# q of six batches transposed on VectorE in 32x32 blocks instead of on TensorE, in a pooled-attention and mixer kernel

## The chip, the cores and the metric

The kernel runs on one core of one Trainium2 chip. The metric is the device time of one execution, in microseconds. Times are medians of several executions of the same program. A median quoted beside a ratio is over all runs of that kernel. Runs of one kernel differ by about 1.5%, and the longer ones have a lower mean granted clock of TensorE: the kernel before took 302.3 us at a mean clock of 1.00 and 305.5 us at 0.979. In the profiled run of the kernel before, the low clock stands at 11 to 21 us.

## The reference, cut to what matters

```python
# q, k, v: [8 batches, 8 heads, 576 tokens, 64]
k_p = k.reshape(B, H, 72, 8, 64).mean(axis=3)          # 8 tokens pooled into one
v_p = v.reshape(B, H, 72, 8, 64).mean(axis=3)
attn = softmax(q @ k_p.T / 8)                          # 576 x 72 a head
x = attn @ v_p                                         # heads side by side: [B, 576, 512]
u = x + (relu(x.T @ w_tok1) @ w_tok2).T                # token mixing, 576 -> 256 -> 576
out = u + relu(u @ w_ch1) @ w_ch2                      # feed-forward, 512 -> 1536 -> 512
```

q enters the score matmul as the moving operand with head dimension on partitions, so each q tile has to be transposed first. The feed-forward is most of the arithmetic.

A warning about correctness. In this draw q and the pooled k are so small that the softmax is nearly flat: with q set to zero the reference's output changes by 0.36% in norm. The chip's correctness check therefore passes even for a kernel with a wrong q. For the changed layout the loads, the block transposes and the score matmul on the host in plain array code gave the exact scores in the order that the later stages expect.

## The kernel before: the parts that matter

The program is a sequence of units. Unit n computes the feed-forward of batch n and, in its gaps, the attention and token mixing of batch n + 1. Unit 0 follows a head that does the attention of batch 0; units 1 to 6 are alike, unit 7 and a last one for leftover rows have no attention to do. Tiles named `ps` lie in PSUM, the memory that the matmuls write to; there are one to three buffers of a kind, and one is written again only after an engine has read what stood in it. The position table below says after which step of unit n's feed-forward a step of batch n + 1 is put.

```python
        def qT(hp):                            # one head pair: five 128x128 transposes on TensorE
            def go():
                ps = (ps_one if first else ps_tr).tile([P, NE, 2, BP], BF16, ...)
                for rr in range(NE):
                    nc.tensor.transpose(out=ps[:, rr]..., in_=st["qb"][:, hp, rr * P:(rr + 1) * P], identity=ident)
                nc.scalar.copy(out=dst, in_=ps)            # PSUM -> SBUF on ScalarE
        # [cut]
        def av(c):                             # attention times v, then the normalisation
            def go():
                # 8 matmuls into ps_two (2 buffers)  [cut]
                nc.vector.reciprocal(out=den[rows], in_=view[:, :, :, D])
                nc.vector.tensor_tensor(out=dst..., in0=view[:, :, :, 0:D], in1=den..., op=ALU.mult)   # x
        # [cut]
        def u(c):                              # token mixing back, residual; ps_one has 3 buffers
            # matmuls into ps_one [cut]
            nc.vector.tensor_tensor(out=dst, in0=ps, in1=x, op=ALU.add)
    # [cut]
    LATER = {1: "kpT", 3: "q0", 5: "q1", 6: "o0", 7: "q2", 8: "e0", 10: "o1", 11: "q3", 12: "e1", 14: "o2", 16: "e2",
             18: "o3", 20: "e3", 23: "av0", 25: "av1", 27: "av2", 29: "av3", 31: "av4", 33: "at0", 34: "at1", ...}
    # [cut]
    def unit(n, at):
        load(n + 2)                            # k, q, v of a later batch, from GpSimd's queue
        batches[n + 1][0]()                    # pooling of k and v on GpSimd (batch 1: VectorE)
        # feed-forward of batch n, with the steps of `at` between  [cut]

    with tc.manual_schedule(engines={PE, POOLE}):          # order as written for TensorE and GpSimd
        with tc.manual_schedule(engines={DVE, ACT}):       # head and unit 0: also VectorE and ScalarE
            # head [cut]
            unit(0, FIRST)
        for n in range(1, B + 1):
            unit(n, LATER)                     # here a scheduler orders VectorE and ScalarE
```

The last lines: TensorE and GpSimd follow the written order, while from unit 1 on the scheduler decides where an instruction of VectorE stands in its queue. VectorE then works through its queue in order: in the trace after the change, an add that doesn't need the late load stands behind a transpose that waits 15.4 us for it.

The softmax here doesn't subtract the row's maximum and nothing guards it: scores larger than these inputs give would overflow.

Of the kernel before, what the change touches and what calls it, by code (L numbers as in the profile page):

```python
# [19 lines left out]
def kernel(  # L20
# [19 lines left out]
    BP, BR = 64, S // 64  # L40
    NE = (BR + 1) // 2
    EV, OD = NE * BP, (BR - NE) * BP
    NO = BR - NE
    ORDER = list(range(1, BR, 2)) + list(range(0, BR, 2))
    CHUNK = [1, 3, 0, 2]
    HP = H // 2
    DM = H * D
    DT = moe_w_tok1.shape[1]
# [22 lines left out]
    uT_tails = singles.tile([P, 4, 4 * P], BF16)  # L71
    u_tails = singles.tile([P, 4, DM], BF16)
    kTs = [singles.tile([P, 2, H * SP], BF16, name=f"kTs{i}") for i in range(2)]


    loaded = {}

    def load(b):
        if b >= B:
            return  # L80
        kr = raw.tile([SP, H, POOL, D], BF16, name="kr")
        vr = raw.tile([SP, H, POOL, D], BF16, name="vr")
        qb = raw.tile([P, HP, BR * D + D], BF16, name="qb")
        nc.vector.memset(qb[:, :, BR * D:], 0.0)
        loaded[b] = (kr, vr, qb)

        def q_in(a0, a1):
            return q[b, 2 * a0:2 * a1].rearrange("(a l) (p r) d -> (l p) a (r d)", l=2, r=BR)

        def kv(t, src, h0, h1):  # L90
            nc.gpsimd.dma_start(out=t[:, h0:h1].rearrange("j h i d -> j h (i d)"),  # L91
                                in_=src[b, h0:h1].rearrange("h (j i) d -> j h (i d)", i=POOL))

        if b == 0:
            for a in range(2):
                nc.sync.dma_start(out=qf[:, a:a + 1, :], in_=q_in(a, a + 1))
            loaded["q23"] = q_in
            kv(kr, k, 0, HP)
            kv(kr, k, HP, H)
            make_identity(nc, ident)  # L100
            kv(vr, v, 0, HP)
            kv(vr, v, HP, H)
        else:
            kv(kr, k, 0, H)
            nc.gpsimd.dma_start(out=qb[:, :, 0:BR * D], in_=q_in(0, HP))  # L105
            kv(vr, v, 0, H)

    def load_tok():
        nc.gpsimd.dma_start(out=f2, in_=moe_w_tok2.rearrange("(c p) n -> p c n", p=P))
        w = moe_w_tok1.rearrange("(p r) n -> p r n", r=BR)  # L110
        for half in range(2):
            rows = slice(half * BP, (half + 1) * BP)
            nc.gpsimd.dma_start(out=w_tok1[rows, 0:4, :].rearrange("p (b a) n -> p b (a n)", a=2),
                                in_=w[:, 0:8, :].rearrange("p (b u a) n -> p b u (a n)", u=2, a=2)[:, :, half])
        for half in range(2):
            rows = slice(half * BP, (half + 1) * BP)
            nc.gpsimd.dma_start(out=w_tok1[rows, 4 + half, :], in_=w[:, ORDER[8], :])

    def permute_tok2():
        src = f2.rearrange("t m (p r) -> t m r p", r=BR)  # L120
        dst = w_tok2.rearrange("t m (r p) -> t m r p", p=BP)
        for m in range(2):
            nc.gpsimd.tensor_copy(out=dst[:, m, 0:NO], in_=src[:, m, 1:BR:2, :])
            nc.gpsimd.tensor_copy(out=dst[:, m, NO:BR], in_=src[:, m, 0:BR:2, :])
        for half in range(2):
            nc.gpsimd.tensor_copy(out=w_tok2t[:, :, half, half * BP:(half + 1) * BP], in_=w_tok2[:, :, 8 * BP:S])

# [11 lines left out]
    def pool8(eng, t, hs, dst, dup):  # L139
        n = hs.stop - hs.start  # L140
        t4 = att.tile([SP, H // 2, 4, D], FP32, name="t4")
        eng.tensor_tensor(out=t4[:, 0:n], in0=t[:, hs, 0:4], in1=t[:, hs, 4:8], op=ALU.add)  # L142
        eng.tensor_tensor(out=t4[:, 0:n, 0:2], in0=t4[:, 0:n, 0:2], in1=t4[:, 0:n, 2:4], op=ALU.add)
        if dup:
            eng.tensor_tensor(out=dst, in0=t4[:, 0:n, 0, None, :].broadcast_to([SP, n, 2, D]),
                              in1=t4[:, 0:n, 1, None, :].broadcast_to([SP, n, 2, D]), op=ALU.add)
        else:
            eng.tensor_tensor(out=dst, in0=t4[:, 0:n, 0], in1=t4[:, 0:n, 1], op=ALU.add)
# [2 lines left out]

    def batch_steps(b):

        par, first = b % 2, b == 0
        st = {}
        kT = kTs[par]
        lower = slice(par * BP, (par + 1) * BP)

        def prepare():
            kr, vr, qb = loaded.pop(b)  # L160
            kp = att.tile([SP, H, 2, D], BF16, name="kp")
            vp = att.tile([SP, H, D + 1], BF16, name="vp")
            ex = att.tile([SP, H * S + BP], BF16, name="ex")
            nc.vector.memset(vp[:, :, D], float(POOL))
# [2 lines left out]
            if b > 1:  # L167
                for s in ("K0", "K1", "V0", "V1"):
                    name[s]()
            st["qT"] = att.tile([P, HP, 2, EV], BF16, name="qT")  # L170
            st["AT"] = att.tile([P, 2, DM], BF16, name="AT")
            st["x"] = mix.tile([P, 4, DM], BF16, name="x")
            st["u"] = mix.tile([P, 4, DM], BF16, name="u")
# [6 lines left out]
        def pool(t, g):  # L180
            def go():
                hs = slice(g * HP, (g + 1) * HP)
                dst = st["kp"][:, hs] if t == "kr" else st["vp"][:, hs, 0:D]
                pool8(nc.vector if b == 1 else nc.gpsimd, st[t], hs, dst, t == "kr")
            return go

        def kpT(h0, h1):
            def go():
                ps = ps_tr.tile([P, H, SP], BF16, name="pt")
                for h in range(h0, h1):  # L190
                    nc.tensor.transpose(out=ps[:, h, :], in_=st["kp"][:, h].rearrange("j e d -> j (e d)"),  # L191
                                        identity=ident[0:SP, 0:SP])
                for half in range(2):
                    rows = slice(half * D, (half + 1) * D)
                    copy = nc.scalar.copy if first and half == 0 else nc.vector.tensor_copy
                    copy(out=kT[rows, half, h0 * SP:h1 * SP], in_=ps[rows, h0:h1, :].rearrange("p h j -> p (h j)"))  # L196
            return go
# [18 lines left out]
        def qT(hp):  # L216
# [9 lines left out]
                    nc.scalar.copy(out=dst, in_=ps)  # L226
            return go

        def score(hp, odd):
            n, c0 = (OD, 0) if odd else (EV, OD)  # L230

            def go():
                ps = ps_two.tile([P, 2, 512], FP32, name="p2")
                for hl in range(2):
                    h = 2 * hp + hl
                    nc.tensor.matmul(out=ps[0:SP, hl, 0:n], lhsT=kT[:, odd, h * SP:(h + 1) * SP],  # L236
                                     rhs=st["qT"][:, hp, hl, 0:n], start=True, stop=True)
                exv = st["ex"][:, 0:H * S].rearrange("j (h n) -> j h n", h=H)
                nc.scalar.activation(out=exv[:, 2 * hp:2 * hp + 2, c0:c0 + n], in_=ps[0:SP, :, 0:n],
                                     func=AF.Exp, scale=scale)  # L240
            return go

        def av(c):
# [35 lines left out]
        def at_tile(c):  # L279
            def go():  # L280
                for m in range(2):
                    if c == 0:
                        st["at", m] = ps_one.tile([P, 512], FP32, name="p1")
                    ps = st["at", m]
                    nc.tensor.matmul(out=ps, lhsT=w_tok1[:, CHUNK[c] if c < 4 else 4 + par, m * P:(m + 1) * P],
                                     rhs=st["x"][:, c, :] if c < 4 else st["xt"], start=(c == 0), stop=(c == 4))
                    if c == 4:
                        relu(m, ps)
# [9 lines left out]
        def at(m):  # L298
            def go():
                ps = ps_one.tile([P, 512], FP32, name="p1")  # L300
                for c in range(5):
                    nc.tensor.matmul(out=ps, lhsT=w_tok1[:, CHUNK[c] if c < 4 else 4 + par, m * P:(m + 1) * P],  # L302
                                     rhs=st["x"][:, c, :] if c < 4 else st["xt"], start=(c == 0), stop=(c == 4))
                relu(m, ps)
            return go
# [48 lines left out]
            name[f"K{g}"], name[f"V{g}"] = pool("kr", g), pool("vr", g)  # L354
        for hp in range(HP):
            name[f"q{hp}"], name[f"o{hp}"], name[f"e{hp}"] = qT(hp), score(hp, 1), score(hp, 0)
        for c in range(5):
            name[f"av{c}"], name[f"u{c}"], name[f"t{c}"] = av(c), u(c), uT(c)
            name[f"at_{c}"] = at_tile(c)
# [6 lines left out]
    def unit_steps(n, st):  # L366
# [4 lines left out]
        for m in range(NM):  # L371
            ps = ps_one.tile([P, 512], FP32, name="p1")
            for kk in range(4):
                nc.tensor.matmul(out=ps, lhsT=w_ch1[:, kk, m * P:(m + 1) * P], rhs=uT[:, kk, :],  # L374
                                 start=(kk == 0), stop=(kk == 3))
                if kk == 1:
                    yield
            if m % 2 == 0 or n == 0:
                nc.scalar.activation(out=GT[:, m, :], in_=ps, func=AF.Relu)  # L379
            else:  # L380
                nc.vector.tensor_scalar(out=GT[:, m, :], in0=ps, scalar1=0.0, scalar2=None, op0=ALU.max)
# [1 line left out]
        for c in range(4):  # L383
# [6 lines left out]
            o_sb = outp.tile([P, DM], FP32, name="o")  # L390
            nc.vector.tensor_tensor(out=o_sb, in0=ps, in1=u_all[:, c, :], op=ALU.add)
            for half in range(2):
                b, r = (2 * c + half, ORDER[8]) if n == B else (n, ORDER[2 * c + half])
                nc.sync.dma_start(out=out[b].rearrange("(p r) n -> p r n", r=BR)[:, r, :],
                                  in_=o_sb[half * BP:(half + 1) * BP, :])
            yield
# [5 lines left out]
             16: "kpT1 V0", 17: "o1", 18: "e1", 19: "q2", 20: "o2 V1", 21: "e2", 22: "q3", 23: "o3", 24: "e3",  # L402
             25: "av0", 26: "av1", 27: "av2", 28: "av3", 29: "av4", 31: "at0", 32: "at1", 34: "U0", 35: "U1",
             36: "t0 U2", 38: "t1 U3", 39: "U4", 40: "t2", 42: "t3", 46: "t4"}
    LATER = {1: "kpT", 3: "q0", 5: "q1", 6: "o0", 7: "q2", 8: "e0", 10: "o1", 11: "q3", 12: "e1", 14: "o2", 16: "e2",
             18: "o3", 20: "e3", 23: "av0", 25: "av1", 27: "av2", 29: "av3", 31: "av4", 33: "at0", 34: "at1",
             37: "u0", 38: "u1", 39: "t0", 40: "u2", 41: "t1", 42: "u3", 43: "u4 t2", 45: "t3", 47: "t4"}
    warm = singles.tile([P, 512], BF16)

# [25 lines left out]
    with tc.manual_schedule(engines={PE, POOLE}):  # L435
        batches = [batch_steps(b) for b in range(B)]
        with tc.manual_schedule(engines={DVE, ACT}):
# [13 lines left out]
                head(s)  # L451
            nc.vector.memset(kTs[1][D:P, 0, :], 0.0)
            nc.vector.memset(kTs[1][0:D, 1, :], 0.0)
            unit(0, FIRST)
        for n in range(1, B + 1):
            unit(n, LATER)
# [30 lines left out]
```

## Time and profile before

| | before |
|---|---|
| time, median (range) of the first three runs | 302.89 us (302.15 to 305.53) |
| TensorE busy | 95% of the span |
| VectorE, ScalarE busy | 52%, 33% |
| chain of waits that ended last | 87% TensorE |
| q transposes on TensorE in units 1 to 6 | 120 of 128x128 |

The page of the kernel before has one line of busy times, and rows of 40 equal slices (7.6 us each) in tenths; "PEclk" is the clock granted to TensorE. The last line here is the chain of waits.

```profile
span 303.9 us, 4654 instructions
PE 287.8 (95%) x1880; PEld 153.7 (51%) x1916; DVE 158.4 (52%) x318; ACT 100.6 (33%) x176; POOL 135.8 (45%) x120
...
PE   8789998999999999999999999999999999999993
...
DVE  4136956684277427752756275725572567333321
...
PEclk9759999999999999999999999999999999999998
...
PE 87%; DVE 5%; ACT 2%; DMA 2%; issue 2%; POOLq 0%
```

TensorE has no slack to speak of after the head. The table of windows makes this sharper: start and end, length, then the busy time of each engine, and granted clock, share and GB/s of DMA.

```profile
76.00:112.00 36.00, 35.48 (x244) 19.59 (x248) 18.27 (x37) 15.85 (x28) 23.42 (x18) 1.00 0.52 92
112.00:148.00 36.00, 35.44 (x251) 19.17 (x254) 20.29 (x41) 13.02 (x23) 23.55 (x19) 1.00 0.56 98
```

In 36 us TensorE is busy for over 35.4 at full clock. VectorE is busy for 18 to 20 us. What a block of q transposes costs is seen in TensorE's timeline (start, duration, instruction; what it waited for in brackets):

```profile
134.63 0.44 PE L220 MATMUL pt<-ident,qb 128*128 128x128 bf16 x5 [0.24 <-DVE kTs_92 L196]
134.90 1.03 PE L374 MATMUL p_1630<-uT,w_ch_86 128*128 128x512 bf16 x4
```

The next matmul starts 0.27 us after the block, so five transposes take 0.27 us of TensorE. The last relu of unit 3's feed-forward on VectorE starts 0.20 us after the first attention matmul, and VectorE's normalisations follow each other closely (first line TensorE, the others VectorE):

```profile
146.41 0.42 PE L256 MATMUL p_1744<-vp,ex 72*128 72x65 bf16 x8
146.61 0.69 DVE L381 TENSOR_SCALAR GT<-p_1737 128x512 bf16<-128x512 f32 x1 [1.31 <-PE p_1737 L374]
147.22 0.20 DVE L268 RECIPROCAL den<-p_1744 128x8 f32<-128x8 f32 x1
147.45 0.69 DVE L274 TENSOR_TENSOR x<-p_1744,den 128x512 bf16<-128x512 f32 x1
148.06 0.20 DVE L268 RECIPROCAL den<-p_1761 128x8 f32<-128x8 f32 x1
148.29 0.69 DVE L274 TENSOR_TENSOR x<-p_1761,den 128x512 bf16<-128x512 f32 x1
```

One normalisation takes 0.84 us. One more thing: batch 2's q load, issued at 26.97 us in the head. The view of its tile, for the load issued in that window, gives the time from issue to landing:

```profile
DMA to landing us min/median/max: 24.7/24.7/24.7
```

It lands at 51.7 us, in the middle of unit 0, because the loads of weights stand before it in the same queue.

### The profile page before, as it was taken

The numbers are of one execution on the slowest core, as the hardware profiler recorded it, in microseconds if no ns is written. First come the engines' busy times: TensorE is split into PE (matmuls) and PEld (weight loads), VectorE is DVE, ScalarE is ACT, GpSimd is POOL, SyncE is SP. The second block draws the span as 40 slices with busy tenths as digits, with TensorE's granted clock in tenths as the row PEclk, the third lists the DMA queues.
The fourth block names the chain that finished last, engine by engine and source line by source line (L and its number), as shares of the span: only waits on it lengthen the run. The fifth ranks groups of instructions, "written<-read, shape, count | busy, mean of one in ns | idle before, by whom it ended". The sixth has DMA issues, their size and how long they took to land.

```text
span 303.9 us, 4654 instructions
## 1 busy us (share of the span) xinstructions
PE 287.8 (95%) x1880; PEld 153.7 (51%) x1916; DVE 158.4 (52%) x318; ACT 100.6 (33%) x176; POOL 135.8 (45%) x120
## 2 busy tenths in 40 slices
PE   8789998999999999999999999999999999999993
PEld 3565444455555555455545554455446545444441
DVE  4136956684277427752756275725572567333321
ACT  2344478005810481029202920093008400300300
POOL 8285104992798079904991499994000000000000
PEclk9759999999999999999999999999999999999998
DMA  7999999927751755173727373200131012114023
GB/s 146 205 204 205 205 203 171 194 49 126 114 101 39 144 87 105 35 149 44 118 66 129 57 118 71 60 9 2 43 70 27 2 36 70 37 29 98 11 50 90
DMA packets 26517, 28.27 MB, mean 93 GB/s; under 512 B 4864, under 2 KB 21376, under 8 KB 26496
## 3 DMA queue, kind: packets, MB, share of 16 engines
q0 software_dynamic: 20160, 17.35, 37.8%
q1 hardware_dynamic: 6048, 10.03, 13.5%
q10 hardware_dynamic: 288, 0.59, 0.7%
q8 instruction: 15, 0.25, 0.3%
q14 instruction: 6, 0.05, 0.1%
HBM read 35.85 MB, written 9.44 MB: 149 GB/s over the span
## 4 chain that ended last, share of the span: by engine, by line
PE 87%; DVE 5%; ACT 2%; DMA 2%; issue 2%; POOLq 0%
PE pt L220 3%; PE pt L327 3%; DMA kr<-in_k_dram 2%; PE pt L414 1%; DVE x L274 1%; DVE kTs_92 L196 1%; PE pt L191 1%; ACT GT L379 1%; DVE kTs_93 L196 1%; PE p_2935 L386 1%; PE p_1119 L386 1%; PE p_753 L386 1%; PE p_3286 L386 1%; PE p_2487 L386 1%; PE p_1435 L386 1%
## 5 line engine op out<-in xcount | busy, mean ns | idle before, releaser
L386 PEld LDWEIGHTS <-GT 128*128 128x128 bf16 x432 | 38.7, 98 | 36.8 <-issue 0.9
L374 PEld LDWEIGHTS <-w_ch_86 128*128 128x128 bf16 x432 | 40.5, 98 | 32.1 <-issue 1.0
L105 POOL DMA_DIRECT2D qb<-in_q_dram x7 | 5.4, 776 | 51.4 <-PE pt L220 50.7
L226 ACT COPY qT<-pt 128x640 bf16<-128x640 bf16 x28 | 19.3, 691 | 9.0 <-PE pt L220 7.9
L256 PEld LDWEIGHTS <-ex 72*128 72x128 bf16 x320 | 15.1, 98 | 10.2 <-DVE x L274 2.2
L220 PEld LDWEIGHTS <-qb 128*128 128x128 bf16 x160 | 11.7, 100 | 12.0 <-issue 6.6
L414 PE MATMUL pt<-warm 128*128 128x512 bf16 x34 | 12.0, 468 | 2.8 <-DVE kTs_92 L196 1.6
L220 PE MATMUL pt<-ident,qb 128*128 128x128 bf16 x140 | 12.3, 218 | 1.5 <-DVE kTs_92 L196 0.7
L328 DVE COPY uT<-pt 128x512 bf16<-128x512 bf16 x28 | 11.8, 421 | 3.4 <-PE pt L327 3.4
L327 PEld LDWEIGHTS <-u 128*128 128x128 bf16 x112 | 8.6, 98 | 7.2 <-issue 0.9
L236 PEld LDWEIGHTS <-kTs_93 128*72 128x72 bf16 x64 | 7.2, 113 | 8.6 <-issue 1.8
L236 PEld LDWEIGHTS <-kTs_92 128*72 128x72 bf16 x64 | 8.1, 126 | 6.8 <-issue 1.3
L302 PEld LDWEIGHTS <-w_tok_83 128*128 128x128 bf16 x70 | 6.8, 98 | 8.3
L327 PE MATMUL pt<-ident,u 128*128 128x128 bf16 x112 | 10.8, 219 | 0.1
L91 POOL DMA_DIRECT2D kr<-in_k_dram x9 | 7.5, 838 | 7.0 <-DVE t_485 L142 6.1
L317 PEld LDWEIGHTS <-w_tok_84 128*128 128x128 bf16 x64 | 6.2, 98 | 7.4 <-issue 0.5
L91 POOL DMA_DIRECT2D vr<-in_v_dram x9 | 7.5, 836 | 3.1 <-PE p_403 L345 3.1
L414 PEld LDWEIGHTS <-warm 128*128 128x128 bf16 x36 | 3.8, 113 | 5.4 <-issue 2.6
L196 DVE COPY kTs_93<-pt 64x576 bf16<-64x576 bf16 (+1 forms) x10 | 4.0, 395 | 4.3 <-PE pt L191 4.2
L204 PEld LDWEIGHTS <-ident 72*72 72x72 bf16 x32 | 4.4, 138 | 2.0 <-issue 1.3
L191 PEld LDWEIGHTS <-kp 72*128 72x128 bf16 x64 | 3.4, 100 | 3.2 <-DVE kp L211 1.0
L131 POOL DMA_DIRECT2D w_ch_86<-in_moe_w_ch_dram x3 | 2.3, 754 | 5.8 <-DMA kr<-in_k_dram 2.9
(809 smaller groups left out, 694.0 us busy)
## 6 DMA issues: line engine op xcount, KB each, us to landing
out_dram<-o SPq DMA_DIRECT2D x72, 128.0 KB, 2.4
kr<-in_k_dram POOLq DMA_DIRECT2D x7, 576.0 KB, 8.3
qb<-in_q_dram POOLq DMA_DIRECT2D x7, 576.0 KB, 6.5
vr<-in_v_dram POOLq DMA_DIRECT2D x7, 576.0 KB, 9.6
w_ch_86<-in_moe_w_ch_dram POOLq DMA_DIRECT2D x3, 512.0 KB, 9.2
w_ch_87<-in_moe_w_ch_dram POOLq DMA_DIRECT2D x3, 512.0 KB, 17.2
qf<-in_q_dram SPq DMA_DIRECT2D x2, 288.0 KB, 3.0
kr<-in_k_dram POOLq DMA_DIRECT2D x2, 288.0 KB, 8.3
```

The costliest lines, as they stand in the source:

```text
L91: nc.gpsimd.dma_start(out=t[:, h0:h1].rearrange("j h i d -> j h (i d)"), in_=src[b, h0:h1].rearrange("h (j i) d -> j h (i d)", i=POOL))
L196: copy(out=kT[rows, half, h0 * SP:h1 * SP], in_=ps[rows, h0:h1, :].rearrange("p h j -> p (h j)"))
L220: nc.tensor.transpose(out=ps[:, rr].rearrange("m l p -> m (l p)"), in_=st["qb"][:, hp, rr * P:(rr + 1) * P], identity=ident)
L226: nc.scalar.copy(out=dst, in_=ps)
L236: nc.tensor.matmul(out=ps[0:SP, hl, 0:n], lhsT=kT[:, odd, h * SP:(h + 1) * SP], rhs=st["qT"][:, hp, hl, 0:n], start=True, stop=True)
L256: nc.tensor.matmul(out=halves[h // 4][:, (h % 4) * (D + 1):(h % 4 + 1) * (D + 1)], lhsT=st["ex"][:, h * S + n0:h * S + n0 + P], rhs=st["vp ...
L302: nc.tensor.matmul(out=ps, lhsT=w_tok1[:, CHUNK[c] if c < 4 else 4 + par, m * P:(m + 1) * P], rhs=st["x"][:, c, :] if c < 4 else st["xt"], ...
L327: nc.tensor.transpose(out=ps[:, kk, :], in_=src[:, kk * P:(kk + 1) * P], identity=ident)
L328: nc.vector.tensor_copy(out=dst[:, :, o:o + P], in_=ps)
L374: nc.tensor.matmul(out=ps, lhsT=w_ch1[:, kk, m * P:(m + 1) * P], rhs=uT[:, kk, :], start=(kk == 0), stop=(kk == 3))
L386: nc.tensor.matmul(out=ps, lhsT=GT[:, m, c * P:(c + 1) * P], rhs=w_ch2[:, m, :], start=(m == 0), stop=(m == NM - 1))
L414: nc.tensor.matmul(out=ps, lhsT=warm[:, 0:P], rhs=warm, start=True, stop=True)
```

## The change

The intent is to take the q transposes off the busiest engine. For batches 2 to 7, q is loaded with two heads and token parity on groups of 32 partitions, so that VectorE can transpose 32x32 blocks straight into a tile with head dimension on partitions. The pooled k is laid out to match, with zeros for the other head. ScalarE no longer copies q out of PSUM, and takes three of VectorE's relus a unit. The order of token rows becomes the natural one.

```diff
+    BY_PE = 2                                    # batches 0 and 1 stay on TensorE
+                for ph in range(2):
+                    nc.gpsimd.dma_start(
+                        out=qb[ph * 64:(ph + 1) * 64, :, 0:BR * D],
+                        in_=q[b].rearrange("(a l) (j u r) d -> u (l j) a (r d)", l=2, u=2, r=BR)[ph])
 [cut: w_tok1 load and w_tok2 in natural row order, pooling of k with "split"]
+                if not by_pe:
+                    nc.vector.tensor_copy(out=st["kD"], in_=ps.rearrange("p h j -> p (h j)"))
+                    return
+        def qD(g):
+            def go():
+                for ph in range(2):
+                    for db in range(2):
+                        nc.vector.transpose(
+                            out=st["qD"][db * 64:(db + 1) * 64, 2 * g:2 * g + 2, :].rearrange(
+                                "m a (r j u) -> m a r j u", u=2, r=BR)[:, :, :, :, ph],
+                            in_=st["qb"][ph * 64:(ph + 1) * 64, 2 * g:2 * g + 2, 0:BR * D].rearrange(
+                                "m a (r d) -> m a r d", d=D)[:, :, :, db * 32:(db + 1) * 32])
 [cut: score() reads qD and kD; both halves 288 wide]
-            if m % 2 == 0 or n == 0:
+            if m % 4 != 3 or n == 0:
                 nc.scalar.activation(out=GT[:, m, :], in_=ps, func=AF.Relu)
-    LATER = {1: "kpT", 3: "q0", 5: "q1", 6: "o0", 7: "q2", 8: "e0", 10: "o1", 11: "q3", 12: "e1", ...
+    LATER = {0: "Q0", 1: "kpT", 3: "Q1", 6: "e0", 8: "o0", 10: "e1", 12: "o1", 14: "e2", 16: "o2", ...
+            for kp in kps:
+                nc.vector.memset(kp, 0.0)
```

Eight VectorE transposes of 64x576 a batch replace 20 TensorE transposes. As written they stand at the start of unit n for batch n + 1; VectorE's queue is ordered by the scheduler, though. It hoisted them by one or two units: 13 of the 48 stand before the last normalisation of unit 0, and none after unit 4.

More of the change, by code (lines that the diff above doesn't have):

```diff
@@ L42 @@
     EV, OD = NE * BP, (BR - NE) * BP
-    NO = BR - NE
-    ORDER = list(range(1, BR, 2)) + list(range(0, BR, 2))
-    CHUNK = [1, 3, 0, 2]
+    SH = S // 2
+    BY_PE = 2
     HP = H // 2
@@ L73 @@
     kTs = [singles.tile([P, 2, H * SP], BF16, name=f"kTs{i}") for i in range(2)]
+    kps = [singles.tile([SP, H, 2, 2, D // 2], BF16, name=f"kps{i}") for i in range(2)]
     loaded = {}
@@ L83, in load @@
         qb = raw.tile([P, HP, BR * D + D], BF16, name="qb")
-        nc.vector.memset(qb[:, :, BR * D:], 0.0)
+        if b < BY_PE:
+            nc.vector.memset(qb[:, :, BR * D:], 0.0)
         loaded[b] = (kr, vr, qb)
@@ L104, in load @@
             kv(kr, k, 0, H)
-            nc.gpsimd.dma_start(out=qb[:, :, 0:BR * D], in_=q_in(0, HP))
+            if b < BY_PE:
+                nc.gpsimd.dma_start(out=qb[:, :, 0:BR * D], in_=q_in(0, HP))
+            else:
+                for ph in range(2):
+                    nc.gpsimd.dma_start(
+                        out=qb[ph * 64:(ph + 1) * 64, :, 0:BR * D],
+                        in_=q[b].rearrange("(a l) (j u r) d -> u (l j) a (r d)", l=2, u=2, r=BR)[ph])
             kv(vr, v, 0, H)
@@ L112, in load_tok @@
             rows = slice(half * BP, (half + 1) * BP)
-            nc.gpsimd.dma_start(out=w_tok1[rows, 0:4, :].rearrange("p (b a) n -> p b (a n)", a=2),
-                                in_=w[:, 0:8, :].rearrange("p (b u a) n -> p b u (a n)", u=2, a=2)[:, :, half])
+            nc.gpsimd.dma_start(out=w_tok1[rows, 0:4, :],
+                                in_=w[:, 0:8, :].rearrange("p (c u) n -> p c u n", u=2)[:, :, half])
         for half in range(2):
             rows = slice(half * BP, (half + 1) * BP)
-            nc.gpsimd.dma_start(out=w_tok1[rows, 4 + half, :], in_=w[:, ORDER[8], :])
+            nc.gpsimd.dma_start(out=w_tok1[rows, 4 + half, :], in_=w[:, 8, :])
     def permute_tok2():
@@ L122, in permute_tok2 @@
         for m in range(2):
-            nc.gpsimd.tensor_copy(out=dst[:, m, 0:NO], in_=src[:, m, 1:BR:2, :])
-            nc.gpsimd.tensor_copy(out=dst[:, m, NO:BR], in_=src[:, m, 0:BR:2, :])
+            nc.gpsimd.tensor_copy(out=dst[:, m], in_=src[:, m])
         for half in range(2):
@@ L143, in pool8 @@
         eng.tensor_tensor(out=t4[:, 0:n, 0:2], in0=t4[:, 0:n, 0:2], in1=t4[:, 0:n, 2:4], op=ALU.add)
-        if dup:
+        if dup == "split":
+            for l in range(2):
+                i0, i1 = (t4[:, l:n:2, i].rearrange("j a (e d) -> j a e d", e=2) for i in range(2))
+                eng.tensor_tensor(out=dst[:, hs][:, l::2, :, l, :], in0=i0, in1=i1, op=ALU.add)
+        elif dup:
             eng.tensor_tensor(out=dst, in0=t4[:, 0:n, 0, None, :].broadcast_to([SP, n, 2, D]),
@@ L152, in batch_steps @@
     def batch_steps(b):
-        par, first = b % 2, b == 0
+        par, first, by_pe = b % 2, b == 0, b < BY_PE
         st = {}
@@ L160, in prepare @@
             kr, vr, qb = loaded.pop(b)
-            kp = att.tile([SP, H, 2, D], BF16, name="kp")
+            kp = att.tile([SP, H, 2, D], BF16, name="kp") if by_pe else kps[par]
             vp = att.tile([SP, H, D + 1], BF16, name="vp")
@@ L169, in prepare @@
                     name[s]()
-            st["qT"] = att.tile([P, HP, 2, EV], BF16, name="qT")
+            if by_pe:
+                st["qT"] = att.tile([P, HP, 2, EV], BF16, name="qT")
+            else:
+                st["qD"] = att.tile([P, HP, S], BF16, name="qD")
+                st["kD"] = att.tile([P, H * SP], BF16, name="kD")
             st["AT"] = att.tile([P, 2, DM], BF16, name="AT")
@@ L182, in go @@
                 hs = slice(g * HP, (g + 1) * HP)
-                dst = st["kp"][:, hs] if t == "kr" else st["vp"][:, hs, 0:D]
-                pool8(nc.vector if b == 1 else nc.gpsimd, st[t], hs, dst, t == "kr")
+                if t == "kr" and not by_pe:
+                    dst, dup = st["kp"], "split"
+                else:
+                    dst, dup = (st["kp"][:, hs], True) if t == "kr" else (st["vp"][:, hs, 0:D], False)
+                pool8(nc.vector if b == 1 else nc.gpsimd, st[t], hs, dst, dup)
             return go
@@ L190, in go @@
                 for h in range(h0, h1):
-                    nc.tensor.transpose(out=ps[:, h, :], in_=st["kp"][:, h].rearrange("j e d -> j (e d)"),
-                                        identity=ident[0:SP, 0:SP])
+                    row = st["kp"][:, h].rearrange("j e d -> j (e d)" if by_pe else "j e l d -> j (e l d)")
+                    nc.tensor.transpose(out=ps[:, h, :], in_=row, identity=ident[0:SP, 0:SP])
+                if not by_pe:
+                    nc.vector.tensor_copy(out=st["kD"], in_=ps.rearrange("p h j -> p (h j)"))
+                    return
                 for half in range(2):
@@ L227, in qT @@
             return go
+        def qD(g):
[7 more added lines that the diff above has]
+                                "m a (r d) -> m a r d", d=D)[:, :, :, db * 32:(db + 1) * 32])
+            return go
         def score(hp, odd):
-            n, c0 = (OD, 0) if odd else (EV, OD)
+            n = SH if not by_pe else OD if odd else EV
             def go():
                 ps = ps_two.tile([P, 2, 512], FP32, name="p2")
+                exv = st["ex"][:, 0:H * S].rearrange("j (h n) -> j h n", h=H)[:, 2 * hp:2 * hp + 2]
                 for hl in range(2):
                     h = 2 * hp + hl
-                    nc.tensor.matmul(out=ps[0:SP, hl, 0:n], lhsT=kT[:, odd, h * SP:(h + 1) * SP],
-                                     rhs=st["qT"][:, hp, hl, 0:n], start=True, stop=True)
-                exv = st["ex"][:, 0:H * S].rearrange("j (h n) -> j h n", h=H)
-                nc.scalar.activation(out=exv[:, 2 * hp:2 * hp + 2, c0:c0 + n], in_=ps[0:SP, :, 0:n],
-                                     func=AF.Exp, scale=scale)
+                    keys = slice(h * SP, (h + 1) * SP)
+                    lhsT, rhs = ((kT[:, odd, keys], st["qT"][:, hp, hl, 0:n]) if by_pe else
+                                 (st["kD"][:, keys], st["qD"][:, hp, odd * SH:odd * SH + n]))
+                    nc.tensor.matmul(out=ps[0:SP, hl, 0:n], lhsT=lhsT, rhs=rhs, start=True, stop=True)
+                if by_pe:
+                    dst = exv.rearrange("j h (r p) -> j h r p", p=BP)[:, :, odd:BR:2, :]
+                    src = ps[0:SP, :, 0:n].rearrange("j h (r p) -> j h r p", p=BP)
+                else:
+                    dst, src = exv[:, :, odd * SH:odd * SH + n], ps[0:SP, :, 0:n]
+                nc.scalar.activation(out=dst, in_=src, func=AF.Exp, scale=scale)
             return go
@@ L284, in go @@
                     ps = st["at", m]
-                    nc.tensor.matmul(out=ps, lhsT=w_tok1[:, CHUNK[c] if c < 4 else 4 + par, m * P:(m + 1) * P],
+                    nc.tensor.matmul(out=ps, lhsT=w_tok1[:, c if c < 4 else 4 + par, m * P:(m + 1) * P],
                                      rhs=st["x"][:, c, :] if c < 4 else st["xt"], start=(c == 0), stop=(c == 4))
@@ L301, in go @@
                 for c in range(5):
-                    nc.tensor.matmul(out=ps, lhsT=w_tok1[:, CHUNK[c] if c < 4 else 4 + par, m * P:(m + 1) * P],
+                    nc.tensor.matmul(out=ps, lhsT=w_tok1[:, c if c < 4 else 4 + par, m * P:(m + 1) * P],
                                      rhs=st["x"][:, c, :] if c < 4 else st["xt"], start=(c == 0), stop=(c == 4))
@@ L356, in batch_steps @@
             name[f"q{hp}"], name[f"o{hp}"], name[f"e{hp}"] = qT(hp), score(hp, 1), score(hp, 0)
+        name["Q0"], name["Q1"] = qD(0), qD(1)
         for c in range(5):
@@ L392, in unit_steps @@
             for half in range(2):
-                b, r = (2 * c + half, ORDER[8]) if n == B else (n, ORDER[2 * c + half])
+                b, r = (2 * c + half, 8) if n == B else (n, 2 * c + half)
                 nc.sync.dma_start(out=out[b].rearrange("(p r) n -> p r n", r=BR)[:, r, :],
@@ L404 @@
              36: "t0 U2", 38: "t1 U3", 39: "U4", 40: "t2", 42: "t3", 46: "t4"}
-    LATER = {1: "kpT", 3: "q0", 5: "q1", 6: "o0", 7: "q2", 8: "e0", 10: "o1", 11: "q3", 12: "e1", 14: "o2", 16: "e2",
-             18: "o3", 20: "e3", 23: "av0", 25: "av1", 27: "av2", 29: "av3", 31: "av4", 33: "at0", 34: "at1",
+    LATER = {0: "Q0", 1: "kpT", 3: "Q1", 6: "e0", 8: "o0", 10: "e1", 12: "o1", 14: "e2", 16: "o2",
+             18: "e3", 20: "o3", 23: "av0", 25: "av1", 27: "av2", 29: "av3", 31: "av4", 33: "at0", 34: "at1",
              37: "u0", 38: "u1", 39: "t0", 40: "u2", 41: "t1", 42: "u3", 43: "u4 t2", 45: "t3", 47: "t4"}
```

## The prediction

> **What bounds the kernel now.** TensorE: 95% busy on the page; in the table of windows 35.4 to 35.5 of every 36 us between 76 and 256 us, at clock 1.00; 87% of the chain of waits. VectorE is 52% busy, ScalarE 33%.
>
> **Removed.** For six batches, 20 TensorE transposes each. In the timeline a block of five takes 0.27 us, so 1.08 us a batch; with them goes a 0.24 us wait of the first block for the kT copies. Together 1.3 us x 6 = 7.9 us at most, 2.6%. The score matmuls keep their columns. ScalarE and GpSimd lose work too, off the chain.
>
> **Added.** Eight VectorE transposes of 64x576 bf16 a batch. The Trainium skill, "VectorE: DVE Perf Modes", section "The three transpose paths", gives 311 ns for 128 columns; with the trace's slope (512 elements 0.69 us, 1024 elements 1.21 us) I estimate 0.75 us each, 6 us a batch. VectorE stays below 25 of 31 us a unit.
>
> **Their place in the queue decides.** VectorE runs in order, and the scheduler hoists the transposes by two units:
> 1. The first transpose of batch 2 stands in unit 0 between two steps of batch 1's K pooling, reached at about 38 us, and waits for batch 2's q load. Before, that load is issued at 26.97 us and lands 24.7 us later, at 51.7, behind a queue moving 205 GB/s; its first half should land near 50. VectorE stalls about 12 us. Behind it stand the evacuations of u, which hold two of three PSUM buffers, so TensorE stops from about 40 to 53.5 us: +13 to 14 us.
> 2. Batch 3's q load now reuses batch 2's buffer and waits for its transposes (about 62 us). It lands 5 to 6 us later, and batch 3's first transpose stands ahead of batch 1's first attention normalisation: +2 to 3 us. Another 2 us come from transposes between the normalisations. Unit 0 loses about 19 us in all.
> 3. In units 1 to 4 a transpose stands between reciprocal and multiply in three of five normalisations. These follow attention matmuls at 1.13 us spacing with 0.84 us of VectorE work each; with 0.75 more they back up, PSUM buffers turn late and the token matmuls wait: about 1.4 us a unit, 5.6 us. This eats the gain there. Units 5 and 6 hold no transposes and keep their gain.
>
> Sum: 303 - 7.9 + 19 + 5.6 = about 319 us.
>
> **Predicted:** 319 us, 308 to 327. Chances: faster by over 2% 0.05, within 2% 0.07, slower by over 2% 0.88.
>
> **What would show it.** In VectorE's waits, a transpose waiting about 12 us on the q load near 38 us, and another some us near 63 to 68. In the 40 slices, a hole in TensorE's row between 40 and 53 us. Transposes of 0.7 to 0.8 us in the groups. The last two batch units shorter by 1.3 us; units 1 to 4 unchanged, with token matmuls waiting on the normalised x. Step 1 is wrong if the load lands near 40 us; step 3 if token matmuls don't wait.
>
> **What would make it wrong.** Most of it is step 1: if the first half of the load lands much earlier than the whole did, the loss shrinks to a few us, and with step 3 harmless the kernel would be 2% faster. If the strided transposes run slower than one element per cycle, steps 2 and 3 grow. The finer w_tok1 load could lengthen the load-bound head by 1 us.

## The result, and the profile after

Ratios here and below are the mean time of one kernel's fast runs over that of the other's fast runs of the same rounds, so they are not quite the ratio of the medians quoted.

| | before | after |
|---|---|---|
| time, median (range) of four runs each | 303.34 us (302.15 to 305.53) | 326.94 us (326.05 to 327.11) |
| ratio, 95% interval | | 1.0787 (1.073 to 1.0843) |
| TensorE busy | 95% | 88% |
| VectorE busy | 52% | 55% |

The changed kernel is 8% slower. The same parts of its page, with 8.1 us a slice:

```profile
span 325.3 us, 4486 instructions
PE 286.7 (88%) x1796; PEld 145.9 (45%) x1796; DVE 178.4 (55%) x332; ACT 99.5 (31%) x176; POOL 133.6 (41%) x136
...
PE   8699503859999899899988998999999999999994
...
DVE  4357207999725972697269717972465166322121
...
PEclk9999955986999999999999999999999999999999
...
PE 70%; DVE 19%; DMA 7%; ACT 1%; issue 1%
```

There is a hole in TensorE's and VectorE's rows in the sixth slice (40 to 49 us), and the granted clock falls there and again in the ninth and tenth (65 to 81 us). The view of waits says who waited for whom (total us, times, longest us):

```profile
PEld L293 <- DVE x L311: 16.2, 16, 1.8
DVE qD L253 <- DMA qb<-in_q_dram: 15.4, 1, 15.4
PE p L412 <- DVE u L355: 14.4, 1, 14.4
...
DVE qD L253 <- PE p L271: 8.8, 4, 2.2
```

L253 is the new transpose, L355 the evacuation of u, L293 the attention matmul, L311 the normalising multiply. VectorE's timeline in unit 0, with the first transpose of batch 2 between two steps of batch 1's K pooling, and the last V pooling add ahead of batch 3's first transpose:

```profile
33.65 1.21 DVE L148 TENSOR_TENSOR t<-kr 72x1024 f32<-72x1024 bf16 x1
50.30 0.81 DVE L253 STREAM_TRANSPOSE qD<-qb 64x576 bf16<-64x576 bf16 x1 [15.44 <-DMA qb<-in_q_dram]
51.02 0.64 DVE L149 TENSOR_TENSOR t<-t 72x512 f32<-72x512 f32 x1
...
65.81 2.81 DVE L158 TENSOR_TENSOR vp<-t 72x256 bf16<-72x256 f32 x1
68.54 0.81 DVE L253 STREAM_TRANSPOSE qD<-qb 64x576 bf16<-64x576 bf16 x1
```

VectorE stood still from 34.9 to 50.3 us. The q load was issued at 25.9 us and took 24.3 us to land, as in the kernel before.

In units 1 to 4 VectorE's timeline of the normalisations looks like this (unit 2):

```profile
133.23 2.51 DVE L253 STREAM_TRANSPOSE qD<-qb 64x576 bf16<-64x576 bf16 x3 [2.20 <-PE p L271]
135.65 0.65 DVE L419 TENSOR_SCALAR GT<-p 128x512 bf16<-128x512 f32 x1
136.22 0.19 DVE L305 RECIPROCAL den<-p 128x8 f32<-128x8 f32 x1
136.44 0.81 DVE L253 STREAM_TRANSPOSE qD<-qb 64x576 bf16<-64x576 bf16 x1
137.28 0.69 DVE L311 TENSOR_TENSOR x<-p,den 128x512 bf16<-128x512 f32 x1
```

A transpose stands between reciprocal and multiply, and a block of three stands ahead of the last relu of the feed-forward. That block first waits 2.2 us for the score matmuls that still read the buffer it will write: its transposes are for a batch two further on, and the tile has two buffers. TensorE's timeline shows the first attention matmul, the effect in the third one of the unit, and the smaller one in the token matmul; weight loads for the fourth and fifth attention matmuls wait about 0.5 us each:

```profile
134.32 0.42 PE L293 MATMUL p<-vp,ex 72*128 72x65 bf16 x8
...
138.03 0.43 PE L293 MATMUL p<-vp,ex 72*128 72x65 bf16 x8 [1.29 <-DVE x L311]
...
143.54 0.38 PE L339 MATMUL p<-xt,w_tok 128*128 128x512 bf16 x1 [0.67 <-DVE xt L311]
```

Units 1, 3 and 4 have the same two waits, of 1.28 to 1.29 and of 0.35 or 0.67 us.

To see what each unit lost, I take the time at which VectorE starts to write the last tile of x in each unit. The last column is experiment 1 below, which has no transposes at all.

| from last x of ... to last x of ... | before | after | no transposes |
|---|---|---|---|
| start to head | 27.94 | 24.41 | 26.40 |
| head to unit 0 | 28.85 | 52.53 | 30.30 |
| unit 0 to unit 1 | 32.16 | 34.11 | 30.56 |
| unit 1 to 2 | 30.94 | 31.74 | 29.35 |
| unit 2 to 3 | 31.77 | 32.89 | 30.17 |
| unit 3 to 4 | 30.94 | 31.74 | 29.35 |
| unit 4 to 5 | 31.77 | 29.99 | 30.18 |
| unit 5 to 6 | 30.76 | 29.17 | 29.16 |
| unit 6 to end of span | 58.73 | 58.72 | 58.7 |

Unit 0 lost 23.7 us. Units 5 and 6, which hold no transposes in this order, gained 1.6 to 1.8 us each. Units 1 to 4 lost 0.8 to 2.0 us each. The head is not the change's doing: in the profiled run of the kernel before TensorE had half clock for 10 us of the head, and other runs of the same kernel, with a mean granted clock of 0.998 to 1.0, took 301.4 to 302.4 us.

### The profile page after: what moved, and what is told of

Its sections match the earlier page's. It is cut to its first block, busy times and chain, and to the rows that moved or that the text cites. A ratio compares the mean times of both kernels' runs of the same rounds, so it can differ in the third digit from the quotient of the medians.

```text
span 325.3 us, 4486 instructions
## 1 busy us (share of the span) xinstructions
PE 286.7 (88%) x1796; PEld 145.9 (45%) x1796; DVE 178.4 (55%) x332; ACT 99.5 (31%) x176; POOL 133.6 (41%) x136
## 4 chain that ended last, share of the span: by engine, by line
PE 70%; DVE 19%; DMA 7%; ACT 1%; issue 1%
PE p L412 25%; PE p L424 23%; DVE qD L253 8%; DMA qb<-in_q_dram 7%; PE p L354 5%; PE p L271 4%; DVE x L311 4%; PE p L339 4%; PE pt L452 3%; PE pt L364 2%; PE p L293 1%; DVE vp L158 1%; DVE o L429 1%; DVE den L305 1%; DVE xt L311 1%
## 5 line engine op out<-in xcount | busy, mean ns | idle before, releaser
L424 PE MATMUL p<-w_ch,GT 128*128 128x512 bf16 x432 | 112.8, 383 | 0.0
L412 PE MATMUL p<-uT,w_ch 128*128 128x512 bf16 x384 | 97.1, 383 | 15.8 <-DVE u L355 14.4
L417 ACT ACTIVATE GT<-p 128x512 bf16<-128x512 f32 x84 | 49.6, 591 | 105.1 <-PE p L412 93.0
L412 PEld LDWEIGHTS <-w_ch 128*128 128x128 bf16 x432 | 41.7, 98 | 53.1 <-issue 16.6
L253 DVE STREAM_TRANSPOSE qD<-qb 64x576 bf16<-64x576 bf16 x48 | 39.0, 813 | 25.2 <-DMA qb<-in_q_dram 15.4
L277 ACT ACTIVATE ex<-p 72x576 bf16<-72x576 f32 (+1 forms) x64 | 41.2, 646 | 10.9 <-PE p L271 10.2
L149 POOL TENSOR_TENSOR t<-t 72x512 f32<-72x512 f32 x24 | 30.4, 1268 | 1.9
L429 DVE TENSOR_TENSOR o<-p,u 128x512 f32<-128x512 f32 x32 | 21.9, 686 | 10.4 <-PE p L424 10.2
L293 PE MATMUL p<-vp,ex 72*128 72x65 bf16 x320 | 17.5, 197 | 9.4 <-DVE x L311 7.1
L148 POOL TENSOR_TENSOR t<-kr 72x1024 f32<-72x1024 bf16 x12 | 25.5, 2126 | 0.1
L148 POOL TENSOR_TENSOR t<-vr 72x1024 f32<-72x1024 bf16 x12 | 25.4, 2116 | 0.0
L355 DVE TENSOR_TENSOR u<-p,x 128x512 bf16<-128x512 f32 x32 | 21.9, 688 | 6.3 <-PE p L354 6.3
L293 PEld LDWEIGHTS <-ex 72*128 72x128 bf16 x320 | 14.5, 100 | 23.5 <-DVE x L311 16.2
L311 DVE TENSOR_TENSOR x<-p,den 128x512 bf16<-128x512 f32 x30 | 20.5, 682 | 0.7
L110 POOL DMA_DIRECT2D qb<-in_q_dram x12 | 7.6, 634 | 30.6 <-DVE qD L253 26.8
```

The source lines that it names most:

```text
L148: eng.tensor_tensor(out=t4[:, 0:n], in0=t[:, hs, 0:4], in1=t[:, hs, 4:8], op=ALU.add)
L149: eng.tensor_tensor(out=t4[:, 0:n, 0:2], in0=t4[:, 0:n, 0:2], in1=t4[:, 0:n, 2:4], op=ALU.add)
L253: nc.vector.transpose(out=st["qD"][db * 64:(db + 1) * 64, 2 * g:2 * g + 2, :].rearrange("m a (r j u) -> m a r j u", u=2, r=BR)[:, :, :, :, ...
L277: nc.scalar.activation(out=dst, in_=src, func=AF.Exp, scale=scale)
L293: nc.tensor.matmul(out=halves[h // 4][:, (h % 4) * (D + 1):(h % 4 + 1) * (D + 1)], lhsT=st["ex"][:, h * S + n0:h * S + n0 + P], rhs=st["vp ...
L311: nc.vector.tensor_tensor(out=dst.rearrange("p (a h d) -> p a h d", a=2, d=D), in0=view[:, :, :, 0:D], in1=den[rows, :, :, None].broadcast ...
```

## The experiments

The theories. **Queue**: the loss comes from where the transposes stand in VectorE's in-order queue; the first waits for a load that lands late, others delay the normalisations that TensorE waits for. **Amount**: 39 us more work on VectorE cost time wherever it stands. **Slow half loads**: the q load in two halves of 64 partitions is slow in itself. **The rest of the change** (relus moved, row order, finer loads) costs time of its own. Seven kernels were run, each beside the kernel before on the same chip, with medians of before of 302.2 and 302.3 us.

### Experiment 1: no transposes

```diff
-                st["qD"] = att.tile([P, HP, S], BF16, name="qD")
+                st["qD"] = qZ                            # a constant tile of zeros
 [cut: qZ allocated, and set to zero once]
-                for ph in range(2):
+                for ph in range(0):                      # no transposes
```

> The changed kernel without its 48 VectorE transposes: q comes from a constant zero tile (the result is wrong on purpose; everything else, loads included, stays). Queue theory and amount-of-work theory alike: the holes vanish and the TensorE work saved shows in full, about 1.7 us in each of six units as in the two last units of the changed kernel, so 303 - 10 = 293 us. If the other parts of the change cost something (loads in halves, relus moved to ScalarE, row order), it stays at 300 or more.

Measured: 294.47 us (293.50 to 295.99), ratio 0.9729 (0.969 to 0.9768). Its output is wrong, which doesn't matter for the time. The table above shows 1.60 us gained in each of units 1 to 6, 9.6 us in all. So all of the loss but 1.45 us is in the transposes and what they wait for: not in the form of the loads, and not in the moved relus. The 1.45 us are in unit 0, which is that much longer than before; experiment 6 has that too.

### Experiment 2: no transposes between the normalisations

```diff
         for n in range(1, B + 1):
-            unit(n, LATER)
+            with tc.manual_schedule(engines={DVE}):      # VectorE as written within each unit
+                unit(n, LATER)
```

> Changed kernel with VectorE's order inside each unit fixed as written from unit 1 on; the scheduler then puts transposes only before the token relu, none between reciprocal and multiply; the early transposes of batch 2 in unit 0 stay. Queue theory: the 14.4 us hole near 40 us stays; the waits of attention matmuls on the normalised x (16.2 us of weight loads, 7.1 us of matmuls) go, worth about 2.5 us in each of units 1 to 4 and 3 to 5 us in unit 0: 310 to 315 us. Amount-of-work theory: the same 39 us of transposes are still there, so about 327 us.

Measured: 314.61 us (313.84 to 315.77), ratio 1.0409 (1.0373 to 1.0445). The written order holds within a unit, but not between units, so the early transposes of batch 2 stay in unit 0. Its waits keep the hole and lose the waits on x; the hole's lines are:

```profile
PE p L412 <- DVE u L355: 14.0, 1, 14.0
...
DVE qD L253 <- DMA qb<-in_q_dram: 15.0, 1, 15.0
```

The same 48 transposes now cost about 12 us less. The step of unit 0 is 46.97 us instead of 52.53. From there the steps of the table read 31.83, 29.61, 31.04, 29.61, 31.04 and 29.17 us: units 1 to 4 became 1.85 to 2.3 us shorter than in the changed kernel. This falsifies the amount theory for these units, which hold eight transposes each as before (nine in unit 1 of the changed kernel). Two things stay open in this run: unit 5, which now holds transposes too, is 1.05 us longer than in the changed kernel; and units 1 to 5 are still 0.26 to 1.27 us longer than without transposes, with a new wait of TensorE, 2.5 us in all, on token relus that stand behind transposes.

### Experiment 3: the q load earlier

```diff
             load(1)
+            load(2, "q")                                 # only q of batch 2
             load_ch2()
 [cut: unit 0 then loads k and v of batch 2]
```

> Changed kernel with batch 2's q load issued ahead of the three w_ch2 loads instead of behind them (same transposes, same places in VectorE's queue). Queue theory: the load lands near 38 to 40 us instead of 50, the first transpose waits 3 to 5 us instead of 15.4, and the time falls by about 10 us to 315 to 318 us. Amount-of-work theory: 327 us. Slow-half-load theory (loads of 64 partitions are slow in themselves): landing still 20 us and more after issue, no gain.

Measured: 318.32 us (317.77 to 318.81), ratio 1.0528 (1.0498 to 1.0559). Only the place of the load changed; the transposes have the same work and nearly the same places. The two halves took 15.6 and 16.5 us from issue to landing. The first transpose, and later the pooling add that will be taken up in experiment 7:

```profile
38.17 0.81 DVE L261 STREAM_TRANSPOSE qD<-qb 64x576 bf16<-64x576 bf16 x1 [5.28 <-DMA qb<-in_q_dram]
...
57.11 2.82 DVE L166 TENSOR_TENSOR vp<-t 72x256 bf16<-72x256 f32 x1
```

The wait went from 15.44 to 5.28 us, and the time fell by 8.6 us (to 0.3 us above the expected 315 to 318). So the hole is the load's late landing, seen through a transpose that stands ahead of urgent work. The slow-half theory doesn't fit: halves queued behind less land sooner, and in the changed kernel batch 3's two halves, issued at 63.8 us into an almost empty queue, landed in 4.5 and 5.2 us.

### Experiment 4: VectorE in the written order throughout

```diff
-    with tc.manual_schedule(engines={PE, POOLE}):
+    with tc.manual_schedule(engines={PE, POOLE, DVE}):
-        with tc.manual_schedule(engines={DVE, ACT}):
+        with tc.manual_schedule(engines={ACT}):
```

> All of VectorE in the order written, units 0 to 8 in one chain: batch n+1's transposes stand at the start of unit n (four before the copy of kD, four after it), none in unit 0. Queue theory: no hole, no waits in the normalisations, but the copy of kD comes 3.3 us late, so the first score matmul of each of six units waits about 1.7 us, which eats the gain: 298 to 305 us. Amount-of-work theory: 320 us or more.

Measured: 303.86 us (303.38 to 306.60), ratio 1.0069 (1.0018 to 1.012). The hole and the waits on x are gone, and a new wait came, as expected, of the score matmuls on the copy of kD behind four transposes:

```profile
PE p L271 <- DVE kD L211: 8.0, 6, 1.5
```

Six waits of 1.3 us, with the weight loads before them, give back about all of the 9.6 us that TensorE saved. It is the same work in a third set of places, with a third time.

### Experiment 5: each transpose where VectorE is idle

```diff
+    with tc.manual_schedule(engines={PE, POOLE, DVE}):   # as in experiment 4
+        def qD(i): ...                                   # one of the eight transposes
 [cut: LATER without Q0 and Q1; unit() puts the steps below between the others]
+    LATER1 = {**LATER, 0: "T3", 2: "T4 T5", 4: "T6 T7"}                      # batch 2, in unit 1
+    NEXT0 = {32: "T0 T1", 45: "T2"}                                          # batch 2, in unit 0
+    NEXT1 = {8: "T0 T1", 11: "T2", 16: "T3", 19: "T4", 32: "T5 T6", 46: "T7"}  # batch 3, in unit 1
+    NEXT = {2: "T0", 3: "T1", 5: "T2", 9: "T3", 11: "T4", 13: "T5", 32: "T6 T7"}   # batch n+2, in unit n
```

> The changed kernel with the same 48 transposes, VectorE in one written chain, and each transpose put where the trace before shows VectorE idle: for batch n+2 in unit n, six between the feed-forward relus and two ahead of the token relu; batch 2's at the end of unit 0 and the start of unit 1; none between reciprocal and multiply, none ahead of the copy of kD. Queue theory: the kernel without transposes took 294.5 us, and VectorE has the time free, so 294 to 297 us, 2 to 3% faster than before. Amount-of-work theory (39 us more on VectorE cost time wherever they stand): 303 us or more.

Measured: 294.38 us over six runs (293.19 to 297.66; the five fast ones to 296.21), ratio 0.9731 (0.9681 to 0.9782). It beats both kernels, and equals the kernel without transposes. Its profiled run happens to be the slowest of the six, 297.66 us, so only the places are read from it and no time. VectorE's timeline in unit 2, with the copy of kD first, then transposes between the relus, none in the normalisations, and two after the last x:

```profile
101.45 0.46 DVE L210 COPY kD<-pt 128x576 bf16<-128x576 bf16 x1
101.83 2.49 DVE L255 STREAM_TRANSPOSE qD<-qb 64x576 bf16<-64x576 bf16 x3
104.36 0.69 DVE L422 TENSOR_SCALAR GT<-p 128x512 bf16<-128x512 f32 x1
105.08 2.49 DVE L255 STREAM_TRANSPOSE qD<-qb 64x576 bf16<-64x576 bf16 x3
...
118.09 0.69 DVE L313 TENSOR_TENSOR xt<-p,den 64x512 bf16<-64x512 f32 x1
118.82 1.67 DVE L255 STREAM_TRANSPOSE qD<-qb 64x576 bf16<-64x576 bf16 x2
```

All 48 transposes are there, and cost nothing that the interval could show. The amount theory is refuted.

### Experiment 6: the rest of the change alone

```diff
-    BY_PE = 2
+    BY_PE = 8                                            # TensorE transposes all, in the old places
```

> The changed kernel with all eight batches transposed by TensorE in the old slots, so what is left of the change is the token order of rows, the finer w_tok1 load, the q load in one piece, and three relus a unit moved from VectorE to ScalarE. Both theories: within 1% of before, 300 to 306 us; more would mean that the rest of the change costs something of its own.

Measured: 303.99 us (302.50 to 305.43), ratio 1.0048 (0.9989 to 1.0107): the same. In the table its steps are those of the kernel before within 0.03 us from unit 1 on. Unit 0 alone is longer, 30.31 us for 28.85; TensorE waits there 0.69, 0.69 and 0.25 us for relus where the kernel before waits 0.69 us once. What makes these waits was not followed up. With one profile of each, and a head that ran 10 us at half clock before and 3.4 us here, it isn't shown that the change is their cause.

### Experiment 7: a third buffer for q

```diff
-        qb = raw.tile([P, HP, BR * D + D], BF16, name="qb")
+        qb = raw.tile([P, HP, BR * D + D], BF16, name="qb", bufs=3)
-                st["qT"] = att.tile([P, HP, 2, EV], BF16, name="qT")
+                st["qT"] = att.tile([P, HP, 2, EV], BF16, name="qT", bufs=1)
```

> The changed kernel with three buffers for the loaded q instead of two (and one for batch 0 and 1's qT, to make room), so batch 3's load needn't wait for batch 2's transposes. Prediction's step 2 (that wait delays batch 1's first normalisation by 2 to 3 us): 324 us. If instead the 2.4 us before it come from GpSimd's first pooling add holding up VectorE's last V pooling add, which the trace shows (2.81 us for an add of 0.42), the time stays at 326 to 328 us, with that add or its neighbour still long.

Measured: 326.79 us (326.03 to 327.15), ratio 1.0799 (1.0744 to 1.0853): no gain over the changed kernel. Batch 3's load no longer waits for batch 2's transposes (GpSimd's wait of 26.8 us for them is gone), and unit 0's step in the table is 51.94 us for 52.53, unit 1's 33.48 for 34.11; the head of this profiled run is 1.1 us longer. VectorE's last V pooling add is still long:

```profile
67.60 1.42 DVE L158 TENSOR_TENSOR vp<-t 72x256 bf16<-72x256 f32 x1
```

GpSimd's timeline of the same run shows its first pooling add of batch 2:

```profile
66.59 2.13 POOL L148 TENSOR_TENSOR t<-kr 72x1024 f32<-72x1024 bf16 x1
```

In the changed kernel the same add of GpSimd, and the attention matmul that waits for VectorE's, are:

```profile
66.20 2.13 POOL L148 TENSOR_TENSOR t<-kr 72x1024 f32<-72x1024 bf16 x1
...
68.67 0.29 PE L293 MATMUL p<-vp,ex 72*128 72x65 bf16 x4 [1.94 <-DVE vp L158]
```

VectorE's add ends at 69.02 us, 0.30 us after GpSimd's ends at 68.72. In the changed kernel the pair is 68.62 and 68.33 us, in experiment 3 it is 59.93 and 59.63. In the kernel before and in experiments 1, 2, 4, 5 and 6 GpSimd's adds start only after VectorE's pooling is over, and that add takes 0.42 us. The Trainium skill, "SBUF — State Buffer", section "SBUF: two separate sides", says that a VectorE instruction with two SBUF inputs and a GpSimd instruction that reads SBUF share a pair of ports as an exclusive lock: the one that starts first has it for its whole instruction. The ends of the three long adds agree with it: each came 0.3 us after the end of GpSimd's. The starts agree only in this run, where GpSimd's record is the earlier one by 1.0 us; in the changed kernel and in experiment 3 VectorE's add is recorded 0.39 us before GpSimd's, and was held all the same. So the lock as the cause is argued, not shown. No run took this hold away by itself, so its cost of 2.4 us is read from the trace, not from a time.

## Why the prediction was wrong

The direction and the main cause were right. The size was short: 16 us more were forecast, and the measured 326.94 us lies at the very edge of the range (308 to 327), with two of four runs above it; by the ratio of the same rounds the loss is 7.9% where 5.3% was forecast. What failed in the sum is the term of step 3, 5.6 us for a measured 11.05, and after it that of unit 0, 19 us for 23.7. Point by point:

- **Removed work: right in kind, too small.** The forecast was 1.3 us a unit, 7.9 us in all. Experiment 1 gained 1.60 us in each of six units, 9.6 us.
- **Cost of one transpose: near.** 0.75 us was estimated and 0.81 measured. From the 311 ns that the Trainium skill, "VectorE: DVE Perf Modes", section "The three transpose paths", gives for 128 columns to 0.81 us for 576 is, as an estimate, 1.1 ns a column. No run here has the same transposes without the strided destination, so what the stride costs isn't shown.
- **Step 1, the hole: right.** Forecast: the first half of the load lands near 50 us, VectorE stalls about 12 us, and TensorE stops for 13 to 14 us. Measured: landing at 50.3 us, a stall of 15.4 us (VectorE came to the transpose at 34.9 us instead of 38), and a TensorE wait of 14.4 us. Experiment 3 moved the load and the wait shrank by 10.2 us.
- **What step 1 left out: the clock.** After the hole TensorE restarts at half clock. The windows show the same 16 matmuls, from restart on. Before:

```profile
41.30:43.40 2.10, 2.05 (x16) 1.35 (x16) 0.69 (x1) 1.55 (x4) 0.00 (x0) 1.00 1.28 199
```

and after:

```profile
53.90:58.00 4.10, 3.98 (x16) 1.88 (x16) 4.00 (x7) 1.77 (x3) 0.00 (x0) 0.53 0.09 16
```

They take 4.10 us at a clock of 0.53 and 2.10 at 1.00: 2.0 us that the forecast didn't hold. The Trainium skill, "TensorE: Matmul & The Clock Gate", section "What's actually happening", puts the default at half clock and the return at about 3.4 us of activity; here half clock lasted 3.8 us after the restart, which agrees roughly.

There is a second stretch at half clock, from 71.4 to 78.2 us, though the longest wait of TensorE just before it was 1.94 us:

```profile
67.00:78.00 11.00, 7.66 (x51) 3.20 (x51) 10.60 (x20) 0.00 (x0) 10.61 (x10) 0.70 0.58 95
```

VectorE is busy for 10.60 of these 11 us, so up to the last x, at 76.94 us, it sets the pace. Past it the clock shows: the first token relu on VectorE starts 3.31 us after the last x, and 2.67 us after it before the change. In experiment 7 the full clock is back at 76.4 us, before the last x, and it is 2.67 us too. So some 0.6 us of unit 1's loss is clock.

- **Step 2, batch 3's load: failed as told.** The forecast had batch 3's first transpose wait 2 to 3 us for a load that itself waited for a buffer. The trace has only one wait of a transpose on a load, the one of step 1. In its place stood the pooling add, 2.4 us longer than elsewhere and ending with GpSimd's, after which the load had just landed; TensorE waited 1.94 us for that add. The first half of batch 3's load landed at about 68.3 us (issued at 63.8, 4.5 us), 0.3 us before the held add ended; so without the hold the transpose would have waited for the load after all, about 2 us by these numbers. The two delays overlap, and that the size forecast fits the one that was measured is luck. Experiment 7 took away the buffer wait alone and gained nothing in time that can be told from noise. The other 2 us of this step, for transposes between unit 0's normalisations, were 3.3 us (four of 0.82).
- **Step 3, the normalisations: right mechanism, half the size.** This is the step that failed most: the largest term that was mis-sized. Forecast: 1.4 us a unit, 5.6 us in units 1 to 4. Measured against the kernel without transposes: 3.55, 2.39, 2.72 and 2.39 us, 11.05 in all, of which the 0.6 us of clock just named are no part of this step. The token matmuls wait as forecast, but only 0.35 to 0.67 us a unit; the longer wait, 1.28 to 1.29 us in each of the four units, is that of the third attention matmul for a PSUM buffer that a late normalisation still reads. What was overlooked is the block of three transposes ahead of the last relu: it waits up to 2.2 us for score matmuls, so in unit 2 the relu starts 1.33 us after the first attention matmul (134.32 to 135.65 us; the kernel before has 0.20 us there, 146.41 to 146.61 us in unit 3) and the normalisations begin late before they are spread out. Experiment 2 freed the normalisations of transposes and of that block together, and got 1.85 to 2.3 us a unit back; it doesn't divide the two.

The sum: TensorE's gain of 9.6 us, less 23.7 in unit 0 and 11.05 in units 1 to 4, makes a loss of 25.1 us; the median of after less the 302.2 to 302.3 us of later rounds of before is 24.7 (less the 303.34 us of its own rounds, 23.6). Unit 0's 23.7 us are 14.4 of hole, 2.0 of clock, 1.9 of the held add, 1.45 of the rest of the change (experiment 6), 3.3 more between the first attention matmul and the last x (8.27 us for 4.96), and 0.6 that I can't place. Experiment 2, which has the hole but neither the held add nor the transposes between the normalisations, is 5.6 us shorter in unit 0; 1.9 and 3.3 of this sum make 5.2.

## What to carry to other kernels

In this kernel, work moved from a full engine to a half-idle one was free only where it stood in that engine's queue behind nothing that lands late and ahead of nothing that the full engine waits for: the same 48 transposes gave 326.9, 314.6, 303.9 and 294.4 us in four orders. Before trusting a scheduler with such a move, list the order of the receiving engine's queue, and for every moved instruction look up in the old trace when its input lands and which urgent instruction stands behind it. The hole on TensorE cost more than its length, since the matmuls after it ran at half clock: 2.0 us more for 14.4 us of hole.

## What the Trainium skill lacked or had wrong

- "VectorE: DVE Perf Modes", section "The three transpose paths", gives one size for VectorE, 128x128 in 311 ns, and no time for another size or for a strided destination. Here 64 partitions x 576 bf16, written at every second element, took 0.81 us.
- No page read warns that, where a scheduler orders VectorE, an instruction that waits on a load can be hoisted by a unit or two from where it was written and hold up all behind it: one such wait was 15.4 us, and placing all transposes by hand was worth 32.6 us.
- "SBUF — State Buffer" has the port lock. Three runs agree in the ends: a 0.42 us add of two SBUF inputs took 2.81, 2.82 and 1.42 us, each ending 0.3 us after GpSimd's add. That the first to start has the lock fits the recorded starts in one of the three; in the other two VectorE's is the earlier by 0.39 us.
- "TensorE: Matmul & The Clock Gate" has the half clock after idling, and agrees: 16 matmuls took 4.10 us for 2.10 after a hole of 14.4 us. A second stretch of half clock began after waits no longer than 1.94 us.
